# Later loads of conversion blocks, eight early blocks, and a first W2 split shared with VectorE

## Chip, cores and metric

One core of one Trainium2 chip runs the whole program. The metric is the device time of one execution in microseconds (us); lower is better.

## What is computed

A chunked attention (4 batches, 8 heads, 576 tokens, head size 64, chunks of 64), a mixture of eight experts whose gate is normalized by eight Sinkhorn rounds, and a gated MLP, one after the other, in fp32:

```python
    attn = softmax(scale * q_c @ k_c.T)          # within chunks of 64
    x = (attn @ v_c) as [2304, 512]
    P = exp(x @ w_gate - max); 8 rounds of row and column normalization
    for e in range(8):
        out += P[:, e:e + 1] * (np.maximum(x @ w1[e], 0.0) @ w2[e])
    h = out @ w_in
    g = h * np.clip(h + 3.0, 0.0, 6.0) / 6.0
    return g @ w_out
```

`w_in` and `w_out` come in as 64-bit floats and are read as pairs of 32-bit words.

## The kernel before

Every fp32 product is made of rounded parts: a matrix is cut into a high and a low part (`cut_piece`: ScalarE copies the high part, another engine subtracts it), and three products of parts are summed in PSUM. The products with an expert's or the MLP's first and second weights are further done as seven block products in place of eight, with sums and differences of blocks ahead and behind.

The program has these stretches. Up to about 277 us: attention, and expert 0 on all six blocks of tokens (`flat`, 48 steps of four hooks each; side work is hung on a hook with `add`). From 277 to about 742 us: experts 1 to 7 on the first third of the tokens, 28 slots (`slots`, each of seven positions, one block product per position; side work is hung on a position with `at_slot`). From 742 to about 1185 us: the second third, 28 slots, now with the second product also as seven blocks ("turned"; `second`), and from there the last third; from about 1600 us the MLP. In a turned position TensorE does six matmuls of the first product and six of the second. The second product's weights come from HBM into a ring of four places, `W2R` (`w2r_load`, L1133); a load is issued when the product that read its place is done. The first product's weights are loaded by `w1_load` (L784).

All loads and stores are issued by SP, in the order in which the program places them, and a load that has to wait holds those behind it.

A **conversion block** is a piece of 128 x 512 of `w_in` or `w_out`: a load of 512 KB (`cv_load`, L184), five operations of VectorE (L202, L211, L214, L217, L220) and two of ScalarE (L205, L208) that make fp32 of the 64-bit numbers (`cv_op`), and a store of 256 KB (`cv_keep`, L227) to `scr_in` or `scr_out` in HBM. There are 32. The first `CV0` are done before 277 us in parts of a fixed tile (`cv_early`, `part_buf`). The others are placed by `book_cv`: a planner searches, from a position on, the next one at which the booked work of VectorE or ScalarE leaves room (`book`). There a block lives in one of two spare buffers (`spare_buf`, each block a new tile in the same place), so the next block's load into it waits until the store of the one before has landed. Its load is placed at `back[b]`, its first operation four positions later or more, its store one position after the last operation. The last four blocks use a fixed tile again, two at a time.

The first slot's second weights are cut in two pieces by `w2_piece` (L882), with the subtraction on GpSimd (L859); the sums of W2 are cut by `w2s_piece`, also on GpSimd.

VectorE empties the PSUM banks of the first product with adds at L979 (bank hb into `p` or `u`, bank hc into `u`); until that is done TensorE can't fill the bank again. Its instructions run in program order.

Of the kernel before, what the change touches and what calls it, by code (L numbers as in the profile page):

```python
# [28 lines left out]
def chunk_attention_moe_mlp(  # L29
# [23 lines left out]
    nc = tc.nc  # L53
# [135 lines left out]
    def part_buf(o):  # L189
        return lambda _: lambda z, n, dt: part(o + z, n, dt)  # L190
# [548 lines left out]
    TURN = ends[FIRST_TURNED - 1]  # L739

    held, user = {0: None, 1: None}, {0: None, 1: None}
    b = 1
    for s in slots:
        if held[b] != s.k:
            b = 1 - b
# [13 lines left out]
    def x_slot(t, i, shape, dt, name):  # L759
        return pools[("X0", "XE")[t]].tile(shape, dt, tag=f"x{t}{i}", name=name)  # L760

    def spare_buf(seg, b, name):
        tile_ = x_slot(*spares[seg][b], [128, 4 * HN], F32, name)

        def buf(o, n, dt):
            v = tile_[:, o:o + n]
            return v if dt is F32 else v.bitcast(dt)

        return buf
# [22 lines left out]
    raw1, raw2 = {}, {}  # L792
# [63 lines left out]
    def cut_piece(hi, lo, r, lo_eng):  # L856

        nc.scalar.activation(out=hi, in_=r, func=AF.Copy)  # L858
        lo_eng.tensor_tensor(out=lo, in0=r, in1=hi.bitcast(F32), op=ALU.subtract)  # L859

    def cut_ops(w, r, o0, o1, lo_eng):

        cut_piece(w[:, o0:o1, 0], w[:, o0:o1, 1], r, lo_eng)
# [15 lines left out]

    W2t = {}  # L880

    def w2_piece(s, z):  # L882
        if z == 0:
            W2t[s.i] = pools["W2"].tile([128, 4, 2, 256], F32R, tag="W2", name=f"W2_{s.i}")
        cut_ops(W2t[s.i], raw2[s.k][:, 2 * z:2 * z + 2], 2 * z, 2 * z + 2, nc.gpsimd)

    SS = {}

# [226 lines left out]
    for s in slots[TURN::2]:  # L1115
        a, b = s, slots[s.i + 1]
# [224 lines left out]
    pos = {s: i for i, s in enumerate(flat)}  # L1341


    with tc.manual_schedule():
# [95 lines left out]
        def add(i, z, fn, *a):  # L1440
            hooks.setdefault(4 * i + z, []).append((fn, a))
# [26 lines left out]
        s = pos[0, 4, 5]  # L1468
# [21 lines left out]
        park(0, pos[0, 1, 1], range(1, 37, 2))  # L1490
        park(1, pos[0, 3, 0], range(2, 38, 2))

        CV0 = 4

        def cv_early(at0, pace):
            for i in range(CV0):
                q, o = at0 + i * pace, i % 2 * 3 * CW
                add(0, q - 7, cv_load, (i,), part_buf(o))
                for x, y in enumerate((0, 3, 3, 6, 7, 9, 11)):
                    add(0, q + y, cv_op, (i,), x)  # L1500
                add(0, q + 13, cv_keep, (i,))

        cv_early(4 * pos[0, 1, 1] + 3, 20)

        def to_right():
            scopes["xs"].close()
# [12 lines left out]
        s = pos[0, 4, 3]  # L1519
# [46 lines left out]
        def at_slot(i, z, fn, *a):  # L1566
            sides.setdefault((7 * i + z) // 7, {}).setdefault((7 * i + z) % 7, []).append((fn, *a))
# [28 lines left out]
        for s in slots:  # L1596
            g = 7 * s.i
# [23 lines left out]
        def book(g, fn, *a, dve=0.0, act=0.0, pool=0.0):  # L1621
            need = (("DVE", dve), ("ACT", act), ("POOL", pool))
            def full(e, c):
                v = load[e]
                if e != "DVE":
                    if g < 7 * TURN + 7:
                        return v[g] + c > CAP[e]
                    return max(sum(v[g - 2:g + 1]), sum(v[g - 1:g + 2]), sum(v[g:g + 3])) + c > 6.05
                old = new = 0.0
                for i in range(max(0, g - 7), g + 8):  # L1630
                    old = max(0.0, old + v[i] - (2.08 if i >= 7 * TURN else 2.23))
                    new = max(0.0, new + v[i] + c * (i == g) - (2.08 if i >= 7 * TURN else 2.23))
                    if new > max(SLACK, old):
                        return True
                return False

            while any(c and full(e, c) for e, c in need):
                g += 1
            use(g, dve, act, pool)
            at_slot(0, g, fn, *a)  # L1640
            return g

        def book_cuts(g, end, pieces):
            for fn, *a in pieces:
                if a[-1] == 3 and fn is w1_piece:
                    g = book(g + 1, fn, *a, nc.vector, act=0.4, dve=0.8)
                else:
                    g = book(g, fn, *a, act=0.62, pool=1.3)
            assert g < end, (g, end, pieces)
            return g  # L1650

        for s in slots[:NEXP]:
            if s.i > 1:
                g = max(7, 7 * (s.i - 2) + 3)
                for n in range(NSUM):
                    g = book(g, w1_sum, s.k, n, dve=1.0 if n == 0 else 0.8)
# [4 lines left out]
            elif s.i:  # L1661
                g = book_cuts(max(g + 1, 7 * (s.i - 1)), 7 * s.i,
                              [(w1_piece, s, z) for z in range(4)])
# [3 lines left out]
        for s in slots[:TURN]:  # L1667
            if s.i:
                at_slot(s.i - 1, 0, raw_load2, s.k)
            g = 7 * s.i  # L1670
            h = book_cuts(g + 1, g + 7, [(w2_piece, s, z) for z in range(2)])
            at_slot(0, h + 2, w2_keep, s)
            for n in range(NSUM):
                g = book(g, w2_sum, s.k, n, dve=1.0 if n == 0 else 0.8)
            h = book_cuts(max(g, h) + 1, 7 * s.i + 8,
                          [(w2s_piece, s.k, z) for z in range(2)])
            at_slot(0, h + 2, w2s_keep, s.k)
# [21 lines left out]
        def book_cv(g, todo, bufs, pace, width, end):  # L1699
            back = [g] * len(bufs)  # L1700
            c = 0
            while todo and max(g, back[c % len(bufs)]) + 13 < end:
                ii = tuple(todo[:width])
                del todo[:width]
                buf, b = bufs[c % len(bufs)], c % len(bufs)
                c += 1
                at_slot(0, back[b], cv_load, ii, buf)
                t = g = max(g, back[b] + 4)
                for x, cost in enumerate(CV_COST):
                    act = x in (1, 2)  # L1710
                    if x in (1, 3):
                        g += 2
                    cost = (cost + 0.45) * len(ii) / 2
                    if len(ii) == 1:
                        cost += 0.22
                    g = book(g, cv_op, ii, x, dve=cost * (not act), act=cost * act)
                at_slot(0, g + 1, cv_keep, ii)
                back[b] = g + 1
                g = max(t + pace, g - 3)
            return g + 6  # L1720

        rest = list(range(CV0, len(cv_list)))
        book_cv(16, rest, [lambda nm, b=b: spare_buf(0, b, nm) for b in range(2)], 12, 1, 7 * TURN - 14)

        kept = {}

        def book_x2(g, p, kl, step):
            for o in (0, 1, 2, 4, 5, 3, 6):
                g = book(g, x2_cut, p, kl, o, act=0.53, pool=1.05)
                at_slot(0, g + 3, x2_keep, p, kl, o)  # L1730
                kept[p, o] = g + 3
                if o == 2:
                    h = g
                    for n in range(4):
                        h = book(h + 1, x2_diff, kl, n, dve=0.7)
                    g = max(g, h - step + 1)
                g += step
            return g
# [23 lines left out]
        g = 7 * ends[0] + 9  # L1762
        for kl in range(2):
            g = book_x2(g, 0, kl, 3)
        g = book_ahead(g + 4, range(NEXP, NEXP + NG4))
        book_cv(7 * ends[0] + 8, rest, [lambda nm, b=b: spare_buf(1, b, nm) for b in range(2)], 8, 1, 7 * ends[1] - 18)
        g = book_cv(g, rest, [part_buf(0)], 0, 2, 7 * ends[1] + 20)
        assert not rest, rest
        for p in (1, 2):
            g = max(g + 2, 7 * ends[p] + 17)  # L1770
            h = 7 * ends[p] + 26
            if p == 1:
# [4 lines left out]
                for kl in range(2):  # L1777
                    for z in range(2):
                        g = book(g, x2_scale, p, kl, z, dve=1.2)
                for kl in range(2):  # L1780
                    g = max(g, h + 4)
                    for z in range(2):
                        g = book(g, x2_add, p, kl, z, dve=1.2)
                    if kl:
                        g = max(g, t)
                    t = book_x2(g + 1, p, kl, 2)
                g = book_ahead(t + 4, range(NEXP + NG4, NSET))
                assert g < 7 * ends[2] + 16, (g, 7 * ends[2])
                continue
            for kl in range(2):  # L1790
                at_slot(0, g, x2_first, p, kl)
                h = max(g + 1, h)
                at_slot(0, h, x2_get, p, kl)
                g += 8
                for fn in (x2_scale, x2_add):
                    for z in range(2):
                        g = book(g, fn, p, kl, z, dve=1.2)
                    g = max(g, h + 4)
                g = book_x2(g + 1, p, kl, 2) + 4
# [73 lines left out]
```

## Time and profile before

| | |
|---|---|
| median of 3 runs | 1945.02 us (1944.7 to 1947.44) |
| profiled execution, its own time | 1950.22 us |
| its span | 1948.1 us |
| TensorE matmuls busy | 1902.0 us (98%) |
| VectorE busy | 1572.3 us (81%) |
| GpSimd busy | 1231.7 us (63%) |
| ScalarE busy | 815.5 us (42%) |
| HBM read and written | 304 GB/s over the span |

The busy time of matmuls counts overlapping pipelined instructions once, so a busy TensorE can still be fed too slowly; the number of matmuls that start in a stretch tells that. A wait is put down to what ended it.

### The profile page before, as it was taken

What the parts mean: (1) busy time and instruction counts of PE and PEld (TensorE: products, weight loads), DVE (VectorE), ACT (ScalarE), POOL (GpSimd) and SP (SyncE); (2) the same over time, 40 slices, a digit from 0 to 9 for tenths busy, and PEclk for the clock granted to TensorE, in tenths of its full rate; (3) what the DMA queues carried; (4) which work ended last, traced back from release to release, by engine and by line L of the source; (5) the groups of instructions that cost most, each with busy time, mean ns of one, the idle gap of its engine ahead of it and who ended that gap; (6) DMA issues with size and microseconds to landing.
All of it is one profiled execution on the core that took longest, in us unless ns stands there. A gap on an engine that the chain in (4) does not pass through costs nothing.

```text
span 1948.1 us, 34479 instructions
## 1 busy us (share of the span) xinstructions
PE 1902.0 (98%) x11915; PEld 1815.7 (93%) x11915; DVE 1572.3 (81%) x2365; ACT 815.5 (42%) x1632; POOL 1231.7 (63%) x1073
## 2 busy tenths in 40 slices
PE   9999999999999999999899999999999999999998
PEld 8789998888888898999898999999999999999998
DVE  6666477788878858989898889898888788798867
ACT  5233236555555534333333333233333335454453
POOL 3223258878887866658786455576888656566543
PEclk9999999999999999999999999999999999999999
DMA  9867579999998997989999898999999999998884
GB/s 215 219 180 206 203 240 388 325 311 332 318 325 308 318 343 267 322 322 342 326 354 341 312 333 294 321 327 327 347 369 362 368 339 335 331 315 302 300 265 149
DMA packets 353661, 594.18 MB, mean 305 GB/s; under 512 B 56512, under 2 KB 171600, under 8 KB 353360
## 3 DMA queue, kind: packets, MB, share of 16 engines
q1 hardware_dynamic: 353488, 591.98, 88.0%
q8 instruction: 95, 1.56, 0.3%
q14 instruction: 78, 0.64, 0.1%
HBM read 405.68 MB, written 186.20 MB: 304 GB/s over the span
## 4 chain that ended last, share of the span: by engine, by line
PE 74%; DVE 11%; DMA 9%; issue 2%; ACT 2%; SPq 1%; POOL 1%; DVEq 0%; ACTq 0%; POOLq 0%
PE o L1195 17%; PE hb L937 13%; PE ha L937 9%; PE o L1185 8%; PE hc L937 8%; PE acc L1077 6%; PE h L587 5%; PE acc L624 5%; DMA W2R<-wsc 3%; DVE r L837 2%; DMA scr_in<-cv 2%; DVE u L979 1%; DMA r<-in_moe_w_dram 1%; DVE r L831 1%; DMA wsc<-W 1%
## 5 line engine op out<-in xcount | busy, mean ns | idle before, releaser
L937 PE MATMUL hb<-X,W 128*128 128x384 f32 x1944 | 392.9, 336 | 4.8 <-DVE u L979 4.2
L937 PEld LDWEIGHTS hb<-X,W 128*128 128x128 f32 x1944 | 339.2, 188 | 16.0 <-DVE u L979 9.3
L1195 PE MATMUL o<-Hb,W2R 128*128 128x384 f32 x1296 | 278.9, 337 | 16.6 <-DMA W2R<-wsc 15.2
L937 PE MATMUL ha<-X,W 128*128 128x384 f32 x1296 | 261.0, 336 | 6.2 <-DVE p L979 5.4
L937 PE MATMUL hc<-X,W 128*128 128x384 f32 x1296 | 263.6, 338 | 1.2 <-DVE u L979 1.0
L1077 PE MATMUL acc<-W,H 128*128 128x512 f32 x1008 | 259.2, 391 | 0.6 <-POOL H L960 0.5
L1195 PEld LDWEIGHTS o<-Hb,W2R 128*128 128x128 f32 x1296 | 230.5, 189 | 20.3 <-issue 16.2
L1220 DVE SCALAR_TENSOR_TENSOR accM<-o,accM 128x768 f32<-128x768 f32 x209 | 198.8, 951 | 49.9 <-PE o L1195 35.6
L937 PEld LDWEIGHTS ha<-X,W 128*128 128x128 f32 x1296 | 225.8, 188 | 10.9 <-issue 7.4
L937 PEld LDWEIGHTS hc<-X,W 128*128 128x128 f32 x1296 | 229.1, 190 | 7.3 <-DVE u L979 2.7
L1195 PE MATMUL o<-Ha,W2R 128*128 128x384 f32 x1056 | 228.2, 335 | 6.2 <-DMA W2R<-wsc 4.8
L859 POOL TENSOR_TENSOR Hb<-u,Hb 128x384 fp32r<-128x384 f32 x144 | 165.9, 1154 | 89.9 <-ACT Hb L858 79.6
L1077 PEld LDWEIGHTS acc<-W,H 128*128 128x128 f32 x1008 | 187.4, 188 | 30.7 <-POOL H L960 3.5
L859 POOL TENSOR_TENSOR W<-r,W 128x512 fp32r<-128x512 f32 (+1 forms) x140 | 194.9, 1426 | 15.4 <-ACT W L858 14.7
L1195 PEld LDWEIGHTS o<-Ha,W2R 128*128 128x128 f32 x1056 | 187.2, 188 | 7.8 <-issue 3.6
L979 DVE TENSOR_TENSOR u<-hc,u 128x384 f32<-128x384 f32 x216 | 118.5, 549 | 47.1 <-PE hc L937 46.5
L859 POOL TENSOR_TENSOR Ha<-t,Ha 128x384 fp32r<-128x384 f32 x89 | 95.8, 1076 | 94.5 <-ACT Ha L858 86.4
L859 POOL TENSOR_TENSOR Hb<-p,Hb 128x384 fp32r<-128x384 f32 x94 | 111.9, 1190 | 65.3 <-ACT Hb L858 44.7
L979 DVE TENSOR_TENSOR u<-hb,p 128x384 f32<-128x384 f32 x216 | 118.5, 549 | 41.7 <-PE hb L937 36.7
L859 POOL TENSOR_TENSOR Ha<-u,Ha 128x384 fp32r<-128x384 f32 x96 | 110.2, 1150 | 51.9 <-ACT Ha L858 50.1
L858 ACT ACTIVATE Hb<-u 128x384 fp32r<-128x384 f32 x144 | 75.5, 524 | 161.2 <-DVE u L675 55.6
L1185 PE MATMUL o<-W2R,Hb 128*128 128x256 f32 x837 | 129.1, 281 | 0.0
(201 smaller groups left out, 3562.2 us busy)
## 6 DMA issues: line engine op xcount, KB each, us to landing
W2R<-wsc SPq DMA_DIRECT2D x280, 512.0 KB, 6.1
W<-wsc SPq DMA_DIRECT2D x504, 256.0 KB, 6.0
wsc<-W SPq DMA_DIRECT2D x28, 1792.0 KB, 8.3
wsc<-SS SPq DMA_DIRECT2D x28, 1024.0 KB, 9.0
wsc<-m SPq DMA_DIRECT2D x112, 256.0 KB, 5.8
r<-in_moe_w_dram SPq DMA_DIRECT2D x84, 256.0 KB, 8.2
wsc<-W SPq DMA_DIRECT2D x28, 768.0 KB, 8.9
X<-xsc SPq DMA_DIRECT2D x21, 768.0 KB, 8.3
```

The lines of the kernel that those rows point to most:

```text
L587: nc.tensor.matmul(out=hps[:, :n], lhsT=w[:, a, kk, :], rhs=xx[:, kk, :], start=(kk == 0 and a == 0 and xx is xh), stop=(kk == KD - 1 and ...
L624: nc.tensor.matmul(out=o, lhsT=w[:, a, c] if turned else hx[:, c], rhs=hx[:, :n] if turned else w[:, a, :], start=(f == 0 and hx is hi and ...
L831: nc.vector.tensor_tensor(out=t[:, 4:6], in0=t[:, 1:3], in1=t[:, 0:1].to_broadcast([128, 2, 2, 128]), op=ALU.subtract,)
L837: nc.vector.tensor_tensor(out=t[:, o], in0=t[:, x], in1=t[:, y], op=op)
L858: nc.scalar.activation(out=hi, in_=r, func=AF.Copy)
L859: lo_eng.tensor_tensor(out=lo, in0=r, in1=hi.bitcast(F32), op=ALU.subtract)
L937: nc.tensor.matmul(out=ps[:, :HN], lhsT=W1t[s.b][:, wo, a, kl, :], rhs=x[:, b, kl, :], start=(start and kl == 0 and a == 0 and b == 0), st ...
L979: nc.vector.tensor_tensor(out=o, in0=ps[b][:, :HN], in1=x, op=ALU.add)
L1077: nc.tensor.matmul(out=o, lhsT=s.Hs[:, fi, hx, t * 128:(t + 1) * 128], rhs=w[:, 0::3, a, :] if fi == 0 else w[:, 1:3, a, :], start=(s.j % ...
L1185: nc.tensor.matmul(out=o[:, t * 256:(t + 1) * 256], lhsT=hs[q][:, b, t * 128:(t + 1) * 128], rhs=w[:, q, a, :], start=(q, a, b) == mm[0] a ...
L1195: nc.tensor.matmul(out=ps[:, d, :HN], lhsT=w[:, q, a, d * 128:(d + 1) * 128], rhs=hs[q][:, b, :], start=(q, a, b) == mm[0] and not again, ...
L1220: nc.vector.scalar_tensor_tensor(out=dst, in0=src, scalar=sc, in1=dst, op0=ALU.mult, op1=ALU.add)
```

## The change

Three places. In `book_cv` the place at which a spare buffer's next load may be issued, `back[b]`, is five positions behind the store instead of the store's own (`g + 6`, with the store at `g + 1`); the blocks placed before 742 us start at position 35 instead of 16 and stand at least 16 positions apart instead of 12. Eight blocks instead of four are done before 277 us, 12 hooks apart instead of 20, so nine instead of 13 remain for 277 to 742 us; the 11 blocks from 742 us on and the last four are the same. And the first slot's second piece of W2 has its subtraction on VectorE, two positions later than before; the pieces of the sums follow it.

```diff
-    def w2_piece(s, z):
+    def w2_piece(s, z, lo_eng=nc.gpsimd):
...
-        cut_ops(W2t[s.i], raw2[s.k][:, 2 * z:2 * z + 2], 2 * z, 2 * z + 2, nc.gpsimd)
+        cut_ops(W2t[s.i], raw2[s.k][:, 2 * z:2 * z + 2], 2 * z, 2 * z + 2, lo_eng)
...
-        CV0 = 4
+        CV0 = 8
...
-        cv_early(4 * pos[0, 1, 1] + 3, 20)
+        cv_early(4 * pos[0, 1, 1] + 3, 12)
...
-            h = book_cuts(g + 1, g + 7, [(w2_piece, s, z) for z in range(2)])
+            if s.i:
+                h = book_cuts(g + 1, g + 7, [(w2_piece, s, z) for z in range(2)])
+            else:
+                h = g + 3
+                at_slot(0, g + 1, w2_piece, s, 0)
+                at_slot(0, h, w2_piece, s, 1, nc.vector)
             at_slot(0, h + 2, w2_keep, s)
...
                 at_slot(0, g + 1, cv_keep, ii)
-                back[b] = g + 1
+                back[b] = g + 6
...
-        book_cv(16, rest, [lambda nm, b=b: spare_buf(0, b, nm) for b in range(2)], 12, 1, 7 * TURN - 14)
+        book_cv(35, rest, [lambda nm, b=b: spare_buf(0, b, nm) for b in range(2)], 16, 1, 7 * TURN - 14)
```

TensorE's instructions stand in the same order in both programs. The three pieces below are of the order of instructions on one engine.

SP, in the stretch from 742 us, at the sixth store of a conversion block there; before:

```order
L927 DMA wsc_15_113<-m 128x512
L227 DMA scr_in<-cv_9338 128x512
L184 DMA cv_10437<-in_moe_w_out_dram 128x1024
L784 DMA W_0_3090<-wsc_8_70 128x512
L1133 DMA W2R<-wsc_5_103 128x1024
```

SP, the same place in the changed kernel:

```order
L927 DMA wsc_15_113<-m 128x512
L227 DMA scr_in<-cv_9621 128x512
L784 DMA W_0_3126<-wsc_8_70 128x512
L1133 DMA W2R<-wsc_5_103 128x1024
L784 DMA W_0_3126<-wsc_8_70 128x512
L927 DMA wsc_15_113<-m 128x512
L784 DMA W_0_3126<-wsc_8_70 128x512
L927 DMA wsc_15_113<-m 128x512
L1133 DMA W2R<-wsc_5_103 128x1024
L784 DMA W_1_3784<-wsc_7_69 128x512 x2
L927 DMA wsc_15_113<-m 128x512
L184 DMA cv_10543<-in_moe_w_out_dram 128x1024
```

The load of the next block has moved behind two loads of W2R and the loads and stores between them.

VectorE in slot 7 of the stretch from 277 us, at the add of bank hb into `p`; before:

```order
L979 TENSOR_TENSOR u_7_4808<-hc_4824,u_7_4808 128x384
L217 SCALAR_TENSOR_TENSOR cv_4296<-cv_4296 128x512
L220 SCALAR_TENSOR_TENSOR cv_4296<-cv_4296 128x512
L979 TENSOR_TENSOR p_7_4742<-hb_4762,p_7_4742 128x384
L979 TENSOR_TENSOR u_7_4769<-hc_4824,u_7_4769 128x384
```

VectorE at the same add in the changed kernel:

```order
L979 TENSOR_TENSOR u_7_4827<-hc_4843,u_7_4827 128x384
L979 TENSOR_TENSOR p_7_4763<-hb_4783,p_7_4763 128x384
L979 TENSOR_TENSOR u_7_4790<-hc_4843,u_7_4790 128x384
L202 TENSOR_SCALAR cv_4487<-cv_4487 128x512
```

The two conversion operations ahead of the add are gone here; a later block's first one stands behind it.

VectorE in slot 0 of that stretch, at the splits of W1 (`W_1`) and, new, of W2 (`W_0`); before:

```order
L954 SCALAR_TENSOR_TENSOR H_3757<-ha_3750,H_3757 128x384
L859 TENSOR_TENSOR W_1_3748<-r_1_3094,W_1_3748 128x2x256
L979 TENSOR_TENSOR u_0_3807<-hb_3770,p_0_3758 128x384
L859 TENSOR_TENSOR W_1_3748<-r_1_3094,W_1_3748 128x256
L979 TENSOR_TENSOR u_0_3807<-hc_3812,u_0_3807 128x384
```

VectorE, the same place in the changed kernel:

```order
L954 SCALAR_TENSOR_TENSOR H_3793<-ha_3786,H_3793 128x384
L859 TENSOR_TENSOR W_1_3784<-r_1_3130,W_1_3784 128x2x256
L979 TENSOR_TENSOR u_0_3836<-hb_3806,p_0_3794 128x384
L859 TENSOR_TENSOR W_1_3784<-r_1_3130,W_1_3784 128x256
L859 TENSOR_TENSOR W_0_3817<-r_0_3517,W_0_3817 128x2x256
L979 TENSOR_TENSOR u_0_3836<-hc_3842,u_0_3836 128x384
```

A split of 512 columns now stands between the adds of hb and of hc.

## Rows read from the trace of the kernel before

**Rows 1.** Table by stretches (us from the start); its columns are in the first row

```profile
core 0: us, PE busy (x) PEld busy (x) DVE busy (x) ACT busy (x) POOL busy (x), PEclk, DMA share, GB/s
0.00:277.00 277.00, 272.34 (x2480) 243.94 (x2481) 173.92 (x452) 95.08 (x198) 84.74 (x83) 1.00 0.74 210
277.00:742.00 465.00, 454.14 (x2261) 404.95 (x2260) 371.24 (x486) 244.68 (x488) 364.49 (x279) 1.00 0.91 320
742.00:1100.00 358.00, 335.27 (x1872) 328.66 (x1872) 319.27 (x436) 133.62 (x280) 252.57 (x229) 0.98 0.91 332
...
1250.00:1600.00 350.00, 350.00 (x2021) 350.00 (x2020) 297.28 (x425) 126.06 (x269) 253.48 (x239) 1.00 0.97 346
...
1500.00:1550.00 50.00, 50.00 (x291) 50.00 (x290) 38.36 (x59) 17.56 (x39) 36.87 (x37) 1.00 1.02 382
```

**Rows 2.** Waits of TensorE, 742 to 1100: us in total, times, longest

```profile
PE o L1195 <- DMA W2R<-wsc: 19.1, 9, 6.2
```

**Rows 3.** Waits of the DMA queue SP, 742 to 1100: us in total, times, longest

```profile
SPq L184 <- DMA scr_in<-cv: 43.1, 7, 7.2
...
SPq L184 <- DMA scr_out<-cv: 11.0, 2, 5.9
```

**Rows 4.** Timelines of SP and TensorE around 953: start, us, what, idle before

```profile
953.35 0.86 SPq L227 DMA_DIRECT2D scr_in<-cv  x1
960.64 0.33 SPq L184 DMA_DIRECT2D cv<-in_moe_w_out_dram  x1
961.06 0.38 SPq L1133 DMA_DIRECT2D W2R<-wsc  x1
...
965.98 0.66 PE L1195 MATMUL o<-Hb,W2R 128*128 128x384 f32 x1 [6.21 <-DMA W2R<-wsc]
```

**Rows 5.** DMA view, 742 to 1100: traffic, then issues with median us to landing

```profile
DMA packets 60256, 118.91 MB, mean 332 GB/s; under 512 B 5658, under 2 KB 19994, under 8 KB 60225
...
W2R<-wsc SPq DMA_DIRECT2D x80, 512.0 KB, 6.9
...
cv<-in_moe_w_in_dram SPq DMA_DIRECT2D x7, 512.0 KB, 3.7
...
scr_in<-cv SPq DMA_DIRECT2D x7, 256.0 KB, 7.3
```

**Rows 6.** Timeline of TensorE at two further waits for W2R

```profile
1030.29 0.41 PE L1195 MATMUL o<-Ha,W2R 128*128 128x384 f32 x1 [3.32 <-DMA W2R<-wsc]
...
1039.49 0.45 PE L1195 MATMUL o<-Ha,W2R 128*128 128x384 f32 x1 [0.64 <-DMA W2R<-wsc]
```

**Rows 7.** TensorE's timeline at 840; table by stretches right behind three waits

```profile
840.39 1.02 PE L1195 MATMUL o<-Hb,W2R 128*128 128x384 f32 x4 [2.07 <-DMA W2R<-wsc]
...
840.00:845.00 5.00, 4.61 (x18) 4.64 (x19) 3.17 (x5) 0.97 (x2) 2.25 (x2) 0.66 0.99 368
...
964.00:972.00 8.00, 6.02 (x22) 6.05 (x23) 1.97 (x3) 0.94 (x2) 2.33 (x3) 0.58 1.00 373
...
1094.00:1098.00 4.00, 4.00 (x16) 4.00 (x16) 0.67 (x2) 0.53 (x1) 1.00 (x1) 0.61 1.04 406
```

**Rows 8.** Waits of TensorE, 277 to 742

```profile
PE ha L937 <- DVE p L979: 5.4, 5, 1.2
```

**Rows 9.** Timelines of VectorE and TensorE at 400 us

```profile
398.84 1.48 DVE L220 SCALAR_TENSOR_TENSOR cv<-cv 128x512 f32<-128x512 f32 x1
...
400.94 0.59 PE L937 MATMUL ha<-X,W 128*128 128x384 f32 x2 [1.00 <-DVE p L979]
```

**Rows 10.** Up to 277: what line L202 waited for; SP's longest waits in total

```profile
  DMA cv<-in_moe_w_in_dram: 3.3, 1
...
SPq L698 <- POOL xc L695: 61.3, 13, 14.6
```

**Rows 11.** Timelines of VectorE and TensorE at 284 us

```profile
282.19 1.45 DVE L859 TENSOR_TENSOR W<-r,W 128x512 fp32r<-128x512 f32 x1
...
284.17 0.44 PE L937 MATMUL hb<-X,W 128*128 128x384 f32 x1 [1.55 <-DVE u L979]
```

## The prediction

> **What bounds the kernel now.** I read the table by stretches first, because the share of the whole span hides where TensorE waits. From 1250 to 1600 us TensorE never pauses: 2021 matmuls in 350 us, 173 ns each [rows 1]. That is what the same two-product loop does when nothing is late. From 742 to 1100 us the same loop issues 1872 matmuls in 358 us [rows 1]; at 173 ns they would take 324 us, so 34 us are lost there, 22.7 of them idle (358 - 335.27). From 277 to 742 us TensorE is idle for 10.9 us, before that for 4.7 [rows 1]. So the kernel is bound by TensorE's issue, and all that a reordering can win lies in these pauses; TensorE's own order is the same in both programs.
>
> The chain of waits then says what ends the pauses of 742 to 1100: 19.1 us in nine waits for the W2R ring to be filled from HBM [rows 2]. The ring has four places and a product of one place lasts two positions of six plus six matmuls, 2 x 12 x 0.173 = 4.2 us. A load is issued when its place has been read, so it has three products, 12.5 us, before its data are wanted. It lands 6.9 us after its issue in this stretch [rows 5]; 5.6 us are to spare. A queue held for longer than that makes TensorE wait.
>
> The DMA queue's own waits show the holder: SP stands before L184, the load of a conversion block, for 43.1 us in seven and 11.0 us in two waits, until the block's earlier store has landed [rows 3]. The tile of the spare buffer is given back only then. One case in full [rows 4]: the store is issued at 953.35, the load behind it not before 960.64, and the W2R load behind that at 961.06. TensorE's matmul that reads it starts at 965.98, after 6.21 us of idling.
>
> **The change, part by part.** Its time is made against the profiled execution, 1950.2 us with a span of 1948.1; the median of the runs, 1945.0, is 5.2 us lower, and I subtract the same sum from it.
>
> (1) *The load behind the store.* It moves from the position of the store to five positions later. A position is 2.08 us here, so the load comes 10.4 us behind the store; the stores from these blocks land after 7.3 us (scr_in) in this stretch [rows 5]. The load finds its buffer free, and the queue goes on to the W2R load at once. Of the nine waits for W2R, two (3.32 and 0.64 us, at 1030 and 1039) do not follow a held load directly [rows 6]; the other seven sum to 19.1 - 4.0 = 15.1 us. Of these I keep 2 us: at 965.98 the store itself landed only as the hold ended, so W2R's data would have been queued behind it anyway. The two others come some 20 us after another such hold, when the queue that it bunched may not have drained; I take 2.5 of 4.0 off. Behind three of the waits (the one of 6.21 us, 2.07 us at 840 and one at 1093) the granted clock falls to its lower level, 1.2 GHz, and windows of 5, 8 and 4 us show 0.66, 0.58 and 0.61 [rows 7]: 5 x 0.34 + 8 x 0.42 + 4 x 0.39 = 6.6 us, of which I take 6. Sum of this part: 13.1 + 2.5 + 6 = 21.6 us. Bounds: above, all of the 34 us lost but the 22.7 - 19.1 = 3.6 of idling that other engines end, 30; below, only half of the seven waits and no clock, some 8. The loads' L202 still stands four positions, 8.3 us, behind the load, which lands in 3.7 us [rows 5]: no new wait on VectorE.
>
> What limits the rest is the traffic: 118.91 MB go through in this stretch, 332 GB/s on average [rows 5], and at 1500 to 1550 us 382 GB/s with TensorE at 50.00 of 50 [rows 1]. At 382 the bytes need 311 us, so the 22 us are to be had. The Trainium skill (DMA: Bandwidth & Descriptors, Specifications) gives a limit of about 358 GB/s of HBM per core; at that the same bytes need 332 us, an estimate from that page, and this part could bring at most 26 us: the sum would stand, and its upper bound of 30 would shrink to 26. The 382 of the row is above the page's figure, so the row decides.
>
> In the stretch from 277 the same holds exist, but no wait of TensorE there ends on a DMA, so their end is worth nothing by itself.
>
> (2) *Eight blocks ahead of 277 us instead of four, nine instead of 13 after it.* In the stretch from 277 the waits of TensorE for VectorE's add that empties bank hb into p are 5.4 us in five [rows 8]. At 400 us, L220 of a conversion block runs 1.48 us just ahead of that add, and TensorE waits 1.00 us for it [rows 9]. In the order of before, two such conversion operations stand directly ahead of this add in 11 slots, and five of these waited; in the order of the change in four slots. 5.4 x 4/11 leaves 2.0: 3.4 us off. Bounds 0 and 7 (most of the 10.9 idle). In the first stretch four blocks more put 20 operations on VectorE and eight on ScalarE, hidden by the time that these have to spare (VectorE is busy for 173.92 and ScalarE for 95.08 of 277 us [rows 1]); if that cover goes, softmax or transposes come late. Two things bound this cost: TensorE is idle 4.7 us there altogether now [rows 1], and one of the four L202 held VectorE for 3.3 us until its load came [rows 10], since SP itself stands 61.3 us before L698 stores [rows 10]; four more blocks at that price are 13 us. I take 1 us lost, near the low end, because that one hold of 3.3 us delayed no matmul: no wait of TensorE in this stretch is as long.
>
> (3) *First W2 split.* The second half moves from GpSimd to VectorE, two positions later, and ScalarE has one piece less ahead of H. Now TensorE waits 1.55 us at 284.17, behind a 1.45 us split of W1 on VectorE [rows 11]. ScalarE's H comes half a microsecond earlier, so this wait shortens a little; a second split of about 1.45 us then stands before the add of hc, and the next wait grows. Bounds: 1.5 us lost, 1 won; I take 0.5 lost.
>
> (4) *What slides.* The last conversion blocks and the transposed x steps from 1190 us on stand three to six positions later. With 5.6 us to spare per W2R load and no pause at all from 1250 to 1600 [rows 1] I price it at nothing, with 2 us either way.
>
> Sum: 21.6 + 3.4 - 1.0 - 0.5 = 23.5 us off. Profiled execution 1950.2 - 23.5 = 1926.7; median 1945.0 - 23.5 = **1921.5**.
>
> **Rivals.** *The queue stays deep.* With a load or store more or less in front, W2R may be late although SP never holds: a DMA share of 0.91 in the stretch [rows 1] leaves little room, and the wait at 1030 is of this kind [rows 6]. Against it stands the 382 GB/s without a pause [rows 1]. Then half of part 1 comes: 1945.0 - 10.8 - 1.9 = 1932. Chance 0.2.
>
> *The hold only moves.* If stores are issued some 3 us later than their position or land in over 10.4 us, SP stands at L184 as before. The stores' 7.3 us median [rows 5] speaks against it. Then only parts 2 and 3 remain: 1943. Chance 0.05, and this one would not be told from no change: a measurement of this kernel tells about 0.2%, 3.9 us.
>
> *Slower, by the first stretch.* Each of eight blocks has an L202 that waits in VectorE's order for a load that SP issues late; behind it stand softmax and the adds. SP's longest single hold before L698 is 14.6 us [rows 10]. It decides once TensorE loses over 23.5 / 8 = 2.9 us per block; at 4.5 us per block 36 us go against 24.5 won elsewhere: 1956. For it speaks the hold of 3.3 us seen in one of four, against it that TensorE did not notice. Chance 0.04.
>
> **How the numbers follow.** My forecast, with part 1 between 14 and 30, has 0.71. Its far end is 30 + 7 + 1 = 38 us off, 1907. The range leaves out the slower case and the hold that moves, and most of that tail: 1911 to 1937, where 1937 is the rival of the deep queue with 5 us lost in the first stretch. Faster by over 0.2%: 0.71 + 0.2 = 0.91; within 0.2%: 0.05; slower: 0.04.
>
> **What would show it.** In the changed profile: no wait of SP at L184 for a store from 742 us on; waits of TensorE for W2R under 6 us there, and no window with a clock under 0.9 at 840 or 964; more than 1950 matmuls in the 358 us from that loop's start. Waits for the add of hb into p at two or three places, not five. In the first stretch TensorE idle under 7 us. I am wrong if W2R waits stay above 10 us without a hold at L184 (the deep queue), if L184 still shows tens of microseconds (the hold moved), or if the loop starts later than 278 us or so (the first stretch).

## The result and the profile after

| | before | changed |
|---|---|---|
| median | 1945.51 us (1944.7 to 1947.44, 4 runs) | **1917.24 us** (1915.93 to 1917.71, 4 runs) |
| profiled execution, its own time | 1950.22 us | 1915.93 us |
| its span | 1948.1 us | 1914.2 us |

The ratio is 0.9852, with a 95% interval of 0.9835 to 0.9869: 28.3 us faster by the medians, where 23.5 were forecast (1921.5). The two profiled executions are 34.3 us apart, 6 more than the medians, because the one of before took longer than all four runs of its median and the one of after is the fastest of its own. Stretches are compared below between these two; whole kernels by their medians.

The table by stretches of the changed kernel, columns as in [rows 1] (behind the length of the stretch stand TensorE's busy us and, in brackets, the matmuls that start):

```profile
0.00:277.00 277.00, 272.38 (x2481) 244.08 (x2482) 188.64 (x472) 100.12 (x207) 86.45 (x83) 1.00 0.78 221
277.00:742.00 465.00, 458.27 (x2295) 411.24 (x2294) 364.57 (x475) 242.59 (x487) 369.38 (x283) 1.00 0.91 317
742.00:1100.00 358.00, 353.88 (x2020) 349.04 (x2019) 348.52 (x468) 141.53 (x293) 266.58 (x240) 1.00 0.97 353
1100.00:1250.00 150.00, 150.00 (x866) 149.78 (x865) 134.49 (x181) 50.51 (x94) 90.44 (x75) 1.00 0.91 321
```

Read the matmul counts against [rows 1]. From 742 to 1100 us 2020 start in place of 1872, 148 more; at the unhindered 0.173 us that is 25.6 us. From 277 to 742 it is 34 more, at this stretch's 465 / 2295 = 0.203 us each 6.9 us. From 0 to 277 nothing changes: 2481 against 2480, idle 4.62 us against 4.66. From 1100 to 1250 12 more start (854 before), 2.1 us. The sum, 34.6 us, is close to the distance of the two profiled executions. By the starts of the same matmuls in both (TensorE's order is unchanged) the four stretches give, in the order of time, 0.2, 6.2, 25.1 and 2.1 us. Behind 1250 us the counts can't be compared, since the changed kernel is some 34 us further on in its work at the same time; the starts of the same matmuls gain nothing more there.

Before, TensorE waited 19.1 us in nine waits for W2R [rows 2], behind 54.1 us in nine holds of SP [rows 3]. These are all waits of TensorE from 742 to 1100 us of the changed kernel (us in total, times, longest):

```profile
PE o L1195 <- ACT accM L1218: 1.4, 1, 1.4
PE o L1195 <- DMA W2R<-wsc: 1.3, 1, 1.3
PE hb L937 <- DVE u L979: 0.6, 2, 0.4
PE o L1195 <- POOL Hb L859: 0.6, 1, 0.6
```

No wait of SP at L184 for the store of a conversion block is left there. Its timeline at the counterpart of [rows 4] shows why: a load of W2R goes out 1.17 us behind the store, two more follow, and the load of the next block comes 10.88 us behind the store without idling.

```profile
936.55 1.08 SPq L227 DMA_DIRECT2D scr_in<-cv  x1
937.72 0.90 SPq L1133 DMA_DIRECT2D W2R<-wsc  x1
...
945.54 0.32 SPq L1133 DMA_DIRECT2D W2R<-wsc  x1
947.43 0.33 SPq L184 DMA_DIRECT2D cv<-in_moe_w_out_dram  x1
```

From 277 to 742 us, where TensorE waited 5.4 us in five waits for the add of hb into `p` [rows 8], none of these is left. The largest group of its waits there is now:

```profile
PE hb L937 <- DVE u L979: 3.9, 6, 1.6
```

### The profile page after: what moved, and what is told of

It is laid out like the page before. It is cut to its first block, busy times and chain, and to the rows that moved or that the text cites. A ratio compares the mean times of both kernels' runs of the same rounds, so it can differ in the third digit from the quotient of the medians.

```text
span 1914.2 us, 34452 instructions
## 1 busy us (share of the span) xinstructions
PE 1892.2 (99%) x11915; PEld 1810.9 (95%) x11915; DVE 1587.4 (83%) x2366; ACT 813.9 (43%) x1632; POOL 1240.1 (65%) x1072
## 4 chain that ended last, share of the span: by engine, by line
PE 85%; DVE 8%; DMA 3%; issue 2%; ACT 1%; POOL 0%; DVEq 0%; SPq 0%; ACTq 0%; POOLq 0%
PE o L1195 18%; PE hb L937 16%; PE ha L937 10%; PE acc L1077 10%; PE hc L937 10%; PE o L1185 9%; PE h L587 5%; PE acc L624 5%; DVE u L979 1%; DMA W2R<-wsc 1%; PE pv_None L439 1%; DVE accM L1220 1%; PE sc_None L351 1%; DVE r L837 1%; DMA wsc<-W 1%
```

## Experiments

Three series of runs, each timed beside the kernel before on the same chip (medians 1948.19, 1946.63 and 1948.53 us), so ratios are what to compare. Theory H is the prediction's: what costs in the stretch from 742 us is SP held at L184 until the store has landed.

**The load alone, later.** The kernel before with one number changed:

```diff
-                back[b] = g + 1
+                back[b] = g + 6
```

> The kernel before with one line changed: the next load of a spare buffer five positions later (g + 6); four early blocks, spacing 12 and the first W2 split as before. Theory H (SP held at L184 made the W2R loads late): SP waits at L184 for no store from 742 us on, TensorE waits under 4 us for W2R there, no clock loss, and the stretch from 277 us keeps its five waits for the add of hb into p; some 25 us faster than before, about 1920 us. Rival V (the gain comes from the conversion blocks taken off VectorE between 277 and 742 us): at most 6 us faster, about 1940 us.

Measured: 1923.6 us, ratio 0.9875 (0.9854 to 0.9896). The first line is its stretch, the others its waits of TensorE, from 742 to 1100 and from 277 to 742 us:

```profile
742.00:1100.00 358.00, 351.62 (x1990) 346.74 (x1989) 340.13 (x463) 141.67 (x293) 264.36 (x239) 0.99 0.97 349
...
PE o L1195 <- DMA W2R<-wsc: 1.0, 2, 0.7
...
PE ha L937 <- DVE p L979: 5.4, 5, 1.2
```

The holds and the waits for W2R go, the five waits for the add stay. This one number is most of the gain: 1.25% of 1.48%.

**The blocks alone, earlier.** The changed kernel with the load back at the store and the split of W2 back on GpSimd:

```diff
-                back[b] = g + 6
+                back[b] = g + 1
```

> The changed kernel with the next load back at the store's position (g + 1) and the first W2 split back on GpSimd, so only eight early blocks and the spacing of 16 are left of the change. Theory H: SP waits some 54 us at L184 between 742 and 1100 us and TensorE 15 to 20 us for W2R as before; the stretch from 277 to 742 us gains 5 to 7 us; about 1939 us. Rival V: most of the 28 us, about 1922 us.

Measured: 1941.82 us, ratio 0.9966 (0.995 to 0.9982). Waits of SP and of TensorE from 742 to 1100 us:

```profile
SPq L184 <- DMA scr_in<-cv: 44.2, 7, 8.5
...
SPq L184 <- DMA scr_out<-cv: 10.9, 2, 5.8
```

```profile
PE o L1195 <- DMA W2R<-wsc: 19.5, 8, 4.7
```

The holds and the waits of [rows 2, 3] are back, and 0.34% remain, about 6.6 us; they come between 277 and 742 us, where 2303 matmuls start, 42 more than before. With the 1.25% of the first run this adds up to 1.59%, within the interval of the whole change: the two parts hardly touch each other.

**The wait, not the load's place.** A rival to theory H is that it matters where the load's traffic lies. In this kernel every DMA stands where it stood before; only the spare buffer's tile is made once, as in the first stretch, so that the next load waits only for those who use the words that it writes. It writes the first 1024 of a row, the store reads the 512 behind them:

```diff
+    fixed = {}
+
...
-        tile_ = x_slot(*spares[seg][b], [128, 4 * HN], F32, name)
+        if (seg, b) not in fixed:
+            fixed[seg, b] = x_slot(*spares[seg][b], [128, 4 * HN], F32, name)
+        tile_ = fixed[seg, b]
```

> The kernel before with the spare buffer's tile made once and used by all its blocks: every load stands in the same place of SP's order as before, but it writes other columns than the store reads, so it needs not wait for the store; L202 of the next block, which writes the stored columns, waits for it on VectorE. Theory H: what matters is the wait alone, so TensorE's waits for W2R fall under 5 us and it is 20 to 25 us faster than before, about 1922 us. Rival S (what matters is where the load stands: directly behind the store its 512 KB go ahead of the W2R load): the W2R waits stay above 10 us, and it comes to 1935 us or more.

Measured: 1925.76 us, ratio 0.9888 (0.9867 to 0.9909). SP's timeline, and TensorE's wait for W2R from 742 to 1100 us (lines are four further down here):

```profile
942.78 0.43 SPq L227 DMA_DIRECT2D scr_in<-cv  x1
943.26 0.99 SPq L184 DMA_DIRECT2D cv<-in_moe_w_out_dram  x1
944.34 0.57 SPq L1137 DMA_DIRECT2D W2R<-wsc  x1
```

```profile
PE o L1199 <- DMA W2R<-wsc: 2.3, 1, 2.3
```

The load goes out 0.48 us behind the store. The matmul that waited 6.21 us before [rows 4] waits these 2.3 us here, against 1.3 in the changed kernel, and behind it the granted clock is 0.73 from 952 to 956 us. So it is the wait that cost nearly all; of the rival, that the place matters, 1 us of waiting and this fall of the clock can remain. Moving the load and taking its wait away are two repairs of one fault.

**How far behind: two positions, and seven.** The changed kernel with `g + 3`, and with `g + 8`:

```diff
-                back[b] = g + 6
+                back[b] = g + 3
```

> The changed kernel with the spare buffer's next load two positions behind the store instead of five (g + 3). Theory H with its margin: two positions are 4.2 us, a store lands after some 7, so SP still stands 2 to 4 us at each L184 (20 to 35 us in total from 742 to 1100 us), which is less than the 5.6 us that a W2R load has to spare; TensorE then waits under 4 us for W2R and the time is within 3 us of the changed kernel, 1917 to 1920 us. Rival (every held microsecond counts in proportion): half the gain of that stretch is lost, about 1929 us.

> The changed kernel with a spare buffer's next load seven positions behind the store instead of five (g + 8). Theory H (what costs is SP held at L184 until the store has landed, and with five positions, 10.4 us, nothing of that hold is left): the time of the changed kernel, 1917, within 3 us, waits of TensorE for W2R in 742 to 1100 at most 3 us, no wait of SP at L184 for a store. Rival M (a margin between the landing of the store and the load matters, as the run with two positions behind, 1923, might say: 19 us of holds left there and 5.8 us slower with only 1.2 us of W2R waits): two more positions bring some 3 us more, 1914. Third way (blocks that follow one another later collide with the work of the next stretch): over 1920.

Measured: two positions behind 1923.04 us, ratio 0.988 (0.9862 to 0.9898); seven behind 1916.87, ratio 0.9848 (0.9833 to 0.9863), the changed kernel's time. With two positions, SP's holds at L184 are 19.1 us in place of 54.1, and TensorE's waits for W2R are nearly gone all the same:

```profile
SPq L184 <- DMA scr_in<-cv: 15.0, 7, 3.8
...
SPq L184 <- DMA scr_out<-cv: 4.1, 2, 3.2
```

```profile
PE o L1195 <- DMA W2R<-wsc: 1.2, 3, 0.6
```

A hold of at most 3.8 us is within the 5.6 us that a W2R load has to spare; that part came as expected. The total did not: 5.8 us slower than the changed kernel, where at most 3 were expected. Its stretch starts 1995 matmuls, 25 fewer, 4.3 us. Of these one place explains some 2.5 us. TensorE's timeline and the granted clock:

```profile
755.57 1.33 PE L1195 MATMUL o<-Ha,W2R 128*128 128x384 f32 x3 [2.23 <-ACT accM L1218]
...
756.00:758.00 2.00, 2.00 (x8) 2.00 (x8) 1.83 (x2) 1.58 (x4) 2.00 (x2) 0.50 0.52 179
758.00:762.00 4.00, 4.00 (x22) 4.00 (x21) 2.49 (x4) 1.65 (x4) 2.64 (x3) 0.89 0.48 157
```

The wait is 0.86 us longer than the changed kernel's (1.37), and behind it the granted clock falls to 0.50, its level of 1.2 GHz: 0.24 (from 752 to 756) + 1.0 + 0.44 = 1.7 us lost. Further 1.6 us stand in waits for VectorE's adds (hb: 2.2 us in five, where the changed kernel has 0.6 in two). The holds are not needed for the fall of the clock: the changed kernel with the split of W2 on GpSimd, further down, has none of them; it waited 2.21 us for the same copy, and its clock fell as well:

```profile
754.00:758.00 4.00, 4.00 (x16) 4.00 (x15) 2.46 (x4) 2.05 (x5) 3.94 (x5) 0.57 0.61 161
```

Whether the remaining holds cause the rest, or single executions differ so by themselves, one profile can't tell; that stays open. Past the landing of the store, more distance brings nothing.

**GpSimd beside VectorE.** The five waits of [rows 8] ended on adds of VectorE that stood behind conversion operations; but of the slots that still have two such operations ahead of the add in the changed kernel, none waits. One of them, VectorE's and then GpSimd's timeline of before:

```profile
526.65 1.31 DVE L211 SCALAR_TENSOR_TENSOR cv<-cv 128x512 uint32<-128x512 uint32 x1
528.00 1.21 DVE L214 TENSOR_SCALAR cv<-cv 128x512 uint32<-128x512 uint32 x1
529.13 0.54 DVE L979 TENSOR_TENSOR p<-hb,p 128x384 f32<-128x384 f32 x1
```

```profile
524.50 2.91 POOL L859 TENSOR_TENSOR SS<-s,SS 128x512 fp32r<-128x512 f32 x2
527.92 1.00 POOL L960 TENSOR_TENSOR H<-u,H 128x384 fp32r<-128x384 f32 x1 [0.51 <-ACT H L959]
```

and the same of the changed kernel:

```profile
524.83 0.67 DVE L211 SCALAR_TENSOR_TENSOR cv<-cv 128x512 uint32<-128x512 uint32 x1
525.53 0.43 DVE L214 TENSOR_SCALAR cv<-cv 128x512 uint32<-128x512 uint32 x1
525.88 0.55 DVE L979 TENSOR_TENSOR p<-hb,p 128x384 f32<-128x384 f32 x1
```

```profile
520.98 3.17 POOL L859 TENSOR_TENSOR SS<-s,SS 128x512 fp32r<-128x512 f32 x2
526.10 1.02 POOL L960 TENSOR_TENSOR H<-u,H 128x384 fp32r<-128x384 f32 x1 [1.95 <-ACT H L959]
```

The same two operations take 2.52 us beside GpSimd's and 1.10 us in its gap (524.15 to 526.10). The eleven slots of before divide in the same way: in six GpSimd works beside the two operations, which take 1.21 to 1.76 us each, and five of these six are the five waits; in the other five GpSimd pauses, the operations take 0.67 and 0.43 us, and none waits. All four slots of the changed kernel are of the second kind. Theory C: VectorE's operations stretch while GpSimd works, and two of them ahead of the add make TensorE wait only then. The test is the kernel before with all 13 blocks in place and less work for GpSimd. The low parts of the sums of W2 are a second ScalarE copy in place of GpSimd's subtraction, so this kernel leaves those low parts out:

```diff
-        cut_ops(SS[k], raw2[k, "s"][:, 2 * z:2 * z + 2], 2 * z, 2 * z + 2, nc.gpsimd)
+        for a in range(2):
+            nc.scalar.activation(out=SS[k][:, 2 * z:2 * z + 2, a],
+                                 in_=raw2[k, "s"][:, 2 * z:2 * z + 2], func=AF.Copy)
```

> The kernel before in which the low parts of the sums of W2 (w2s_piece) are a second copy on ScalarE instead of a subtraction on GpSimd; the low parts are left out of the computation in this way, and GpSimd has two operations of 1.48 us less in each of the 28 slots. All 13 conversion blocks stay between 277 and 742 us. Theory C (VectorE's operations take twice as long beside GpSimd, and that alone makes the add of hb into p late): L211 and L214 ahead of the add take 0.7 and 0.4 us, the five waits of TensorE for that add, 5.4 us, fall to one or none, and the kernel is 4 to 6 us faster than before. Rival D (too many conversion operations stand ahead of the add): four or five waits and 4 us or more of them stay.

Measured: 1934.0 us, ratio 0.9938 (0.9919 to 0.9957), 12 us, at least twice the 4 to 6 us expected. All five waits for the add of hb into `p` are gone; the largest group of TensorE's waits from 277 to 742 us is the first line, and the second its stretch:

```profile
PE hb L939 <- DVE u L981: 1.6, 1, 1.6
...
277.00:742.00 465.00, 460.71 (x2325) 417.29 (x2324) 318.61 (x499) 279.50 (x554) 288.12 (x232) 1.00 0.93 329
```

VectorE does more operations than before (499 against 486) in 318.61 us against 371.24. Groups of VectorE by line and shape in this stretch, last the mean in ns (before the bar) and idle time behind it; first before:

```profile
L837 DVE TENSOR_TENSOR r<-r 128x256 f32<-128x256 f32 x52 | 61.6, 1184 | 1.5
...
L979 DVE TENSOR_TENSOR p<-hb,p 128x384 f32<-128x384 f32 x29 | 15.9, 547 | 5.0 <-PE hb L937 5.0
...
L211 DVE SCALAR_TENSOR_TENSOR cv<-cv 128x512 uint32<-128x512 uint32 x13 | 14.3, 1099 | 0.0
```

then with less of GpSimd:

```profile
L837 DVE TENSOR_TENSOR r<-r 128x256 f32<-128x256 f32 x52 | 26.4, 508 | 1.6
...
L981 DVE TENSOR_TENSOR p<-hb,p 128x384 f32<-128x384 f32 x30 | 16.7, 556 | 19.2 <-PE hb L939 19.2
...
L211 DVE SCALAR_TENSOR_TENSOR cv<-cv 128x512 uint32<-128x512 uint32 x13 | 9.4, 724 | 0.0
```

1184 ns become 508, 1099 become 724, and the add out of PSUM keeps its 550. Theory C holds. It expected too little because it counted the five waits alone: by the starts of the same matmuls 12.3 us are won between 277 and 742 us, 6.3 of them at the five waits and most of the rest at smaller ones.

**Thirteen blocks again after 277 us.** The changed kernel with the old spacing, so that none is left for the fixed tile at the end:

```diff
-        book_cv(35, rest, [lambda nm, b=b: spare_buf(0, b, nm) for b in range(2)], 16, 1, 7 * TURN - 14)
+        book_cv(16, rest, [lambda nm, b=b: spare_buf(0, b, nm) for b in range(2)], 12, 1, 7 * TURN - 14)
```

> The changed kernel, eight early blocks and the late loads, but blocks from position 16 on and 12 positions apart as before, so 13 blocks again between 277 and 742 us and none left for the fixed tile after 1100 us. Theory: the waits for the add of hb into p come back, some 5 us between 277 and 742 us, and the rest is as in the changed kernel: 1921 to 1924 us. Rival (the gain of that stretch came from the load's place or the split of W2, not from fewer blocks): within 2 us of the changed kernel.

Measured: 1928.06 us, ratio 0.9904 (0.9887 to 0.9921), 10 to 11 us slower than the changed kernel; the direction was right, the size too small. Its waits of TensorE for this add and its stretch from 277 us are those of before, although eight blocks are done early:

```profile
PE ha L937 <- DVE p L979: 5.4, 5, 1.2
...
277.00:742.00 465.00, 452.96 (x2256) 404.16 (x2255) 368.32 (x484) 244.44 (x487) 361.64 (x278) 1.00 0.92 320
```

39 matmuls fewer than in the changed kernel start there, 7.9 us; 22 fewer (844) start from 1100 to 1250 us, 3.8 us, and why was not tried. So the early blocks win nothing by being early; they win by leaving room after 277 us, and by where the blocks that remain come to stand.

**The split of W2, and ten blocks early.** The changed kernel with the first split of W2 as before (both pieces on GpSimd); with `CV0 = 10`, ten hooks apart, and `book_cv(35, …, 20)`; and with both edits.

> The changed kernel with the first W2 split back on GpSimd at its old place. My forecast priced the moved split at 0.5 us lost, so this one should be the same as the changed kernel within a microsecond, 1916 to 1918 us. Rival: the moved split is part of what was won after 277 us, then it is 2 us or more slower, 1919 us or above.

> The changed kernel with ten early blocks ten hooks apart, and seven blocks 20 positions apart between 277 and 742 us. Theory: VectorE has time to spare ahead of 277 us, so the first stretch loses under 1 us, and two blocks less after it win 1 to 2 us: 1915 to 1917 us. Rival: the early blocks now hold VectorE at L202 or make softmax late, and it is 2 us or more slower, 1919 us or above.

> The changed kernel with ten blocks instead of eight ahead of 277 us (ten hooks apart, seven left for 277 to 742 us, 20 positions apart) and the first split of W2 on GpSimd alone, as before the change: the two edits that came out level with the changed kernel (1916.7 each), together. If each is worth a little that its run could not tell (the split 0.5 us in the changed kernel's disfavour, two blocks fewer beside the adds 0.5 us), 1916, between 1914 and 1918. If the first stretch loses what the second wins, 1917. If the split on GpSimd stands beside more conversion work of VectorE at 277 us and doubles its operations, 1919 or more.

Measured: 1916.71 us (ratio 0.984, 0.9821 to 0.986), 1916.7 (0.985, 0.9833 to 0.9866) and 1917.63 (0.9846, 0.9832 to 0.986). None can be told from the changed kernel by its time. The stretch behind the split can tell more, TensorE busy first; the changed kernel, then the same with the split on GpSimd:

```profile
277.00:340.00 63.00, 59.40 (x297) 52.75 (x296) 45.85 (x64) 37.23 (x75) 50.47 (x39) 1.00 0.92 326
```

```profile
277.00:340.00 63.00, 60.75 (x305) 54.15 (x304) 48.81 (x65) 38.22 (x77) 53.17 (x41) 1.00 0.94 335
```

In all five profiles with the split on VectorE, TensorE is busy for 59.4 to 59.6 us here, with it on GpSimd, in the kernel before and in five runs, for 60.2 to 60.8 (the run with less of GpSimd's work is left aside): the moved split costs about 1.3 us, which the scatter of whole times hides. Two more early blocks win nothing that is measured. No version tried is measurably faster than the change.

## Why the prediction was right, point by point

The figures of the parts are those of the two profiled executions. They sum to 6 us more than the medians differ by, and which part holds these 6 us can't be told; so each may be read a little high.

- **What bounds the kernel** was right: the held queue, and TensorE's lost time from 742 to 1100 us.
- **Part 1, 21.6 us** forecast: 25.6 by the two profiles, and 24 by the first experiment's ratio (1.25%, 0.0104 to 0.0146 of 1945 us, 20 to 28). The term that was short is the residue: I kept 2 of the 15.1 us because the data would queue behind the landing store, and 1.5 of the 4.0 us of the two other waits. Measured is one wait of 1.3 us in all, at the matmul that waited 6.21 us before; that is 2.2 of the 4.0 us; the rest lies in smaller waits and in the clock. The clock's 6.6 us counted up to 1.2 twice, since its windows at 840 and 964 us hold 2.4 us of idling [rows 7] that stand in the nine waits already. No window at 840 or 964 us has a lower clock, as forecast.
- **What limits the rest**: the stretch now moves 353 GB/s on average, against 332. I took [rows 1]'s 382 over the 358 of the Trainium skill (DMA: Bandwidth & Descriptors, Specifications), by which at most 26 us could come; 25.6 came, so the sum can't tell the two apart. The traffic in 40 equal slices of the stretch can: 24 of them lie above 358, up to 412, so here the page's figure is no ceiling.

```profile
GB/s 390 284 368 386 404 366 365 290 237 394 406 353 290 346 294 335 376 386 408 370 388 240 368 410 393 389 394 408 285 390 389 412 409 406 295 354 353 259 256 287
```

- **Part 2, 3.4 us after 277 us**: 6.9 by the profiles, about 6.6 by the second experiment. This step's mechanism was incomplete, not only its size off. It counted slots with two conversion operations ahead of the add and scaled 5.4 by 4/11; all five waits went, because it took GpSimd at work beside these operations to make them, and the four slots that remain all stand in its pauses. That the change put them there was not foreseen: it is luck. The upper bound, 7, holds for the 6.9, which has the loss of part 3 in it; with the split on GpSimd (the second experiment) 42 more matmuls start, by the profiles 8.5 us, which is above it.
- **Part 2, 1.0 us lost before 277**: 0 lost. The bound from one L202 of 3.3 us did not recur: VectorE's eight L202 wait for a load once, for 0.3 us.
- **Part 3, 0.5 us lost**: by whole times nothing can be told; by the stretch from 277 to 340 us 1.3 lost, near the bound of 1.5. I priced the second split at 1.45 us, the row of a split beside GpSimd [rows 11]. In the changed kernel GpSimd is done with its three pieces at 282.89 us, and VectorE's two splits of this shape, from 282.02 on, take 2.1 us together, 1.41 and 0.68; TensorE's wait in this place stays as it was ([rows 11], 1.55). So neither the price nor the place of the loss was right: the loss comes in three waits behind it, from 290 to 312 us (0.5, 0.6 and 0.8 us in the changed kernel; with the split on GpSimd two of 0.3):

```profile
L859 DVE TENSOR_TENSOR W<-r,W 128x512 fp32r<-128x512 f32 x2 | 2.1, 1044 | 0.0
...
283.95 1.31 PE L937 MATMUL hb<-X,W 128*128 128x384 f32 x6 [1.57 <-DVE u L979]
```

- **Part 4, nothing**: 2.1 us won from 1100 to 1250 us, inside the 2 either way but for 0.1. The load alone starts 867 matmuls there, 13 more than before, the blocks alone 856, 2 more: it goes with part 1; why was not tried.
- **Rivals.** A queue that stays deep: W2R waits of 1.3 us say no. A hold that only moves: stores were issued in place and landed in 6.3 us (median), some 4 us ahead of the load. A slower first stretch: no loss. The middle of the forecast was 4.3 us too high: the residue of part 1 was smaller, the loss before 277 us did not come, and the waits for the add went altogether, against which the split of W2 cost more. The range was hit with most misses on one side; that they stay this small is in part luck.

## What to carry to other kernels

A DMA queue that issues in order turns one buffer's release into a wait of everything behind it: look for loads that wait on a store, and either let them come later than the store lands or make the wait unnecessary; once the load comes behind the landing, further distance is worth nothing. Price an operation of VectorE by what GpSimd does at that moment, not by its own mean: the same line read 0.67 and 1.31 us. And scale a wait by its cause, which can stand in the timeline of another engine, not by how many instructions stand ahead of it.

## What the runs showed of the hardware

VectorE's operations between SBUF tiles take up to nearly three times as long while GpSimd runs: at 128x256 508 ns in the mean with less of GpSimd's work and 1184 with all of it, L214 0.43 and 1.21 us in the timelines above; adds that read PSUM kept 547 to 556 ns. The Trainium skill (SBUF — State Buffer, SBUF: two separate sides) says that an operation of VectorE with two inputs in SBUF, or in a mode that uses two ports, and one of GpSimd that reads SBUF share a pair of ports: whichever starts first holds it for its whole instruction, and the other blocks. The timelines are near to that: L214 starts at 528.00, GpSimd's H ends at 528.92, and 0.43 us more would be 529.35; it ended at 529.21. L214 has one input in SBUF, and whether it ran in such a mode no trace shows.

TensorE waits at about 755 us for ScalarE's copy `accM`, which stands in ScalarE's order behind an operation (L694) that writes a buffer `m` and first waits until an earlier store of `m` to `x2sc` has landed: for 2.26 us in the changed kernel, 3.13 with two positions behind, 4.00 with the load alone. It is the same fault once more, a release by a store's landing. TensorE's wait was between 0.8 and 2.9 us in the profiles, and it has a second price. After 1.37 us in the changed kernel the granted clock stayed at 1.00; after 2.23 us with two positions behind, shown above, it fell to 0.50, that is 1.2 GHz. The same in the run of the load alone, TensorE's timeline and then the table by stretches:

```profile
761.42 1.33 PE L1195 MATMUL o<-Ha,W2R 128*128 128x384 f32 x3 [2.94 <-ACT accM L1218]
...
762.00:766.00 4.00, 4.00 (x14) 4.00 (x13) 2.00 (x3) 1.83 (x4) 4.00 (x4) 0.50 0.42 113
766.00:770.00 4.00, 4.00 (x20) 4.00 (x20) 2.69 (x5) 1.64 (x3) 1.57 (x3) 0.82 0.86 321
```

4 x 0.50 + 4 x 0.18 = 2.7 us are lost to the clock in these eight, on top of a wait that is 1.6 us longer than the changed kernel's: part of why the load alone stands 6 us behind it. The length of the idling alone does not decide: behind the 2.07 us of [rows 7] the clock fell, behind the 3.32 us of [rows 6] it stayed at 1.00:

```profile
1030.00:1034.00 4.00, 3.71 (x21) 3.74 (x22) 0.56 (x1) 0.00 (x0) 1.81 (x3) 1.00 1.04 377
```
